# A fixed order table for every engine, and one store per output tile, in a gated-attention and token-mixer kernel

## The chip, the cores and the metric

The kernel runs on one core of a Trainium2 chip. The metric is device time in microseconds (us), taken as the median of several executions. A profile adds a span, which runs from the first to the last instruction and is 1.5 to 2 us shorter than the time. On one core, a run more than 1.5% above the fastest of the same kernel is called slow, and ratios use fast runs alone.

Five engines appear in the traces: PE (matrix products, with its weight loads as PEld), DVE (VectorE), ACT (ScalarE), POOL (GpSimd) and SP, which only issues transfers. The program gives each engine its own list of instructions, in a fixed order; an instruction that waits holds up those listed after it. In the trace of the kernel before, ACT idles 2.11 us until an alpha load has landed at 39.6 us, and a copy listed after the operation that needs it starts only at 40.08 us, though the transposes that it reads ended on PE at 38.6 us.

## The reference, cut to what matters

```python
# attention: 4 batches, 8 heads, 768 steps, head size 48; all float32
for t in range(S):
    state = alpha[:, :, t, :, None] * state + np.einsum('bhd,bhe->bhde', k[:, :, t], v[:, :, t])
    y[:, :, t] = np.einsum('bhd,bhde->bhe', q[:, :, t], state)
# mixer on x = y as (4, 768, 384); w_tok 768x256 and 256x768, w_ch 384x1536 and 1536x384
h = np.maximum(x.transpose(0, 2, 1) @ w_tok1, 0.0) @ w_tok2
u = x + h.transpose(0, 2, 1)
out = u + np.maximum(u @ w_ch1, 0.0) @ w_ch2          # (4, 768, 384), float32
```

## The kernel before

The recurrence is computed in 12 blocks of 256 steps (`n` = 0 to 11, three to a batch). Every block loads four 384 KB tiles (alpha, k, q, v). Two neighbouring steps lie in one partition of a load, so a 128-row output tile comes out with the even rows in partitions 0 to 63 and the odd rows in partitions 64 to 127. The store has to undo that.

The program is built as a list of operations with names, possible engines, assumed durations and predecessors. `Plan.once` simulates them with a priority rule and thereby fixes the order on each engine, the engine where there is a choice (DVE or POOL, ACT or DVE), and the buffers:

```python
kk = O("kk", either(dve(768), pool_tt(768)), 5, writes=[pkk], reads=[kt, IE], ...)   # k times decay
trq = O("trq", pe([64] * 8), 8, writes=[bq], reads=[pkq], preds=[qq], emit=lambda e: g.tr(bq, pkq), mode="R")
evq = O("evq", either(dve(1024, True), act(1024)), 9, writes=[tpq], reads=[bq], ...) # copy out of PSUM
# ... t1, t2: token layer; up, ut: transpose of u; c1, c2: channel layer, 288 matmuls of 384 columns each
oo = P.op(f"o_{b}_{i}", dve(384), ..., writes=[o_], reads=[bank, us[i][0]], preds=[prev],
          emit=lambda e, i=i, bank=bank, o_=o_: g.oadd(o_, bank, us[i][0]))
P.op(f"st_{b}_{i}", {"SP": (350.0, 350.0)}, ..., reads=[o_], preds=[oo], emit=lambda e, i=i, o_=o_: g.store(o_, b, i), ...)

def store(self, o, b, i):
    dst = self.out[b, i * 128 : (i + 1) * 128, :].rearrange("(t s) d -> s t d", s=2)
    for h in range(2):
        self.nc.sync.dma_start(dst[h], self.t(o)[64 * h : 64 * h + 64, :])
```

There are three output buffers (`"o": 3`). Input loads and output stores are issued from SP, and weights, which are cast to bf16 on the way, from POOL.

## Time and profile before

| | value |
|---|---|
| time | 191.56 us (189.38 to 192.55, 3 runs) |
| span of the profiled run | 190.1 us |
| PE, DVE, ACT, POOL busy | 86%, 59%, 53%, 19% |
| first channel matmul | 40.9 us |
| last matmul starts | 184.8 us |

The first lines are from the page of the kernel before. The engine line gives busy us and instructions. The lines of digits show the busy share of each fortieth of the span in tenths, for PE, for PE's granted clock and for the transfer engines. The next two lines give the shares of the chain of work that ended last. Then come the group of output adds, with what the engine waited for just before them, and the stores with their time from issue to landing.

```profile
PE 164.0 (86%) x2489; PEld 101.7 (53%) x2489; DVE 112.8 (59%) x197; ACT 101.2 (53%) x200; POOL 35.9 (19%) x43
...
PE   0578578769999988977999999989999999999990
...
PEclk9999999978999999999999999999999999999997
DMA  5999999999999998999100123110001132000243
...
PE 62%; DMA 16%; SPq 10%; DVE 6%; ACT 2%; issue 2%; DVEq 0%; ACTq 0%
PE ps L794 26%; PE ps L799 21%; DMA at<-in_alpha_dram 14%; SPq L562 10%; PE ps L617 7%; PE ps L770 3%; DMA out_dram<-o 2%; DVE u L779 2%; PE ps L775 2%; PE ps L673 2%; DVE pkk L658 1%; DVE pkq L658 1%; DVE o L803 1%; PE ps L786 1%; DVE gtm 
...
L803 DVE TENSOR_TENSOR o<-ps,u 128x384 f32<-128x384 f32 x24 | 13.1, 555 | 38.1 <-PE ps L799 36.2
...
out_dram<-o SPq DMA_DIRECT2D x48, 96.0 KB, 2.2
...
```

PE is the engine that the chain runs through, and it is nearly full from the tenth slice on. The output adds wait 1.8 us for stores in the whole run, and a 96 KB store lands 2.2 us after its issue. The stores cost little here.

Two pieces of the chain of work of the kernel before follow, in order of time (start, length, what):

```profile
20.53 19.10 DMA at<-in_alpha_dram
...
40.91 4.11 PE ps L794 x15
...
```

An alpha load issued at 20.5 us lands at 39.6 us behind the weights. The channel matmuls (L794) start at 40.9 us.

The stretch view (busy us of PE, PEld, DVE, ACT and POOL, each with its count; granted clock; share of the 16 transfer engines; GB/s) over the last stores of the kernel before:

```profile
177.00:189.00 12.00, 8.11 (x50) 4.68 (x48) 3.03 (x6) 0.00 (x0) 0.00 (x0) 0.93 0.41 98
...
```

A share of 0.41 is 6.6 of the 16 transfer engines on average, while stores come in bursts.

### The profile page before, as it was taken

The page shows a single profiled execution, that of the slowest core. Times are in us where ns is not written, and L with a number is a line of the kernel's source. Part 1 is how long each engine was busy: PE and PEld are TensorE (multiplying, and loading weights), DVE is VectorE, ACT ScalarE, POOL GpSimd, SP SyncE. Part 2 cuts the span into 40 slices and gives each one's busy share as a digit, 9 for nine tenths or more (in the row PEclk, how much of TensorE's full clock was granted, in tenths as well). Part 3 has the DMA queues.
Part 4 walks back from the last instruction along what each step waited for, and adds up shares of the span by engine and source line. Part 5 has one row for each costly group of instructions (what it writes and reads, how often), then busy time and mean ns, then how long its engine had stood idle before and what let it go on. Part 6 is the DMA issues. An engine that isn't in the chain of part 4 may idle for free.

```text
span 190.1 us, 5770 instructions
## 1 busy us (share of the span) xinstructions
PE 164.0 (86%) x2489; PEld 101.7 (53%) x2489; DVE 112.8 (59%) x197; ACT 101.2 (53%) x200; POOL 35.9 (19%) x43
## 2 busy tenths in 40 slices
PE   0578578769999988977999999989999999999990
PEld 0357354445566544644566656655656566656650
DVE  3386996993598954869782672894724728100230
ACT  3655536456998624783985212679872121895000
POOL 4023980030431221255200000090000000000000
PEclk9999999978999999999999999999999999999997
DMA  5999999999999998999100123110001132000243
GB/s 156 322 320 270 240 209 207 205 203 270 283 295 247 288 299 229 298 264 269 47 3 3 41 54 75 41 47 5 3 0 40 46 86 71 12 3 0 65 100 83
DMA packets 57625, 27.11 MB, mean 143 GB/s; under 512 B 50816, under 2 KB 57600, under 8 KB 57600
## 3 DMA queue, kind: packets, MB, share of 16 engines
q1 hardware_dynamic: 53760, 23.60, 48.3%
q0 software_dynamic: 3840, 3.15, 10.3%
q8 instruction: 19, 0.31, 0.7%
q14 instruction: 6, 0.05, 0.1%
HBM read 25.17 MB, written 4.72 MB: 157 GB/s over the span
## 4 chain that ended last, share of the span: by engine, by line
PE 62%; DMA 16%; SPq 10%; DVE 6%; ACT 2%; issue 2%; DVEq 0%; ACTq 0%
PE ps L794 26%; PE ps L799 21%; DMA at<-in_alpha_dram 14%; SPq L562 10%; PE ps L617 7%; PE ps L770 3%; DMA out_dram<-o 2%; DVE u L779 2%; PE ps L775 2%; PE ps L673 2%; DVE pkk L658 1%; DVE pkq L658 1%; DVE o L803 1%; PE ps L786 1%; DVE gtm L698 1%
## 5 line engine op out<-in xcount | busy, mean ns | idle before, releaser
L794 PE MATMUL ps<-ut,wc 128*128 128x384 bf16 x288 | 52.8, 333 | 3.3 <-DVE o L803 1.4
L799 PE MATMUL ps<-wc,rt 128*128 128x384 bf16 x288 | 52.5, 327 | 0.0
L765 ACT ACTIVATE rt<-ps 128x384 bf16<-128x384 f32 x93 | 45.1, 490 | 10.9 <-PE ps L794 10.6
L794 PEld LDWEIGHTS <-wc 128*128 128x128 bf16 x288 | 26.9, 99 | 21.5 <-issue 3.7
L799 PEld LDWEIGHTS <-rt 128*128 128x128 bf16 x288 | 26.8, 98 | 17.2
L803 DVE TENSOR_TENSOR o<-ps,u 128x384 f32<-128x384 f32 x24 | 13.1, 555 | 38.1 <-PE ps L799 36.2
L698 DVE TENSOR_TENSOR gtm<-ps,mk 128x1024 bf16<-128x1024 f32 x24 | 28.5, 1218 | 2.3 <-PE ps L617 2.2
L779 DVE TENSOR_TENSOR u<-ps,x 128x384 bf16<-128x384 f32 x24 | 12.7, 552 | 2.0 <-PE ps L775 2.0
L602 POOL TENSOR_TENSOR at<-at 128x384 f32<-128x384 f32 x6 | 6.0, 996 | 33.8 <-DMA at<-in_alpha_dram 22.2
L683 ACT CAST x<-ps 128x384 bf16<-128x384 f32 x16 | 7.2, 479 | 8.1 <-PE ps L617 8.1
L617 PE MATMUL ps<-la,u 128*128 128x384 bf16 x18 | 6.5, 432 | 5.8 <-ACT la L611 5.2
L658 DVE TENSOR_TENSOR pkq<-qt,E 128x768 bf16<-128x768 f32 x10 | 11.0, 1097 | 1.0 <-ACT E L636 1.0
L658 DVE TENSOR_TENSOR pkk<-kt,IE 128x768 bf16<-128x768 f32 x8 | 8.3, 1033 | 4.7 <-ACT IE L642 4.5
L770 PE MATMUL ps<-x,wt 128*128 128x384 bf16 x48 | 10.6, 355 | 0.0
L775 PE MATMUL ps<-ht,wt 128*128 128x384 bf16 x48 | 9.8, 326 | 0.4 <-ACT ht L765 0.4
L673 PE MATMUL ps<-idn,pkk 64*128 64x64 bf16 x192 | 5.5, 202 | 5.4 <-DVE pkk L658 3.1
L617 PE MATMUL ps<-tpq,tpk 48*64 48x128 bf16 x384 | 9.6, 242 | 0.4 <-DVE tpq L685 0.4
L658 POOL TENSOR_TENSOR pkq<-qt,E 128x768 bf16<-128x768 f32 x2 | 3.6, 1810 | 31.8 <-PE ps L673 31.8
L617 PEld LDWEIGHTS <-tpk 48*64 48x64 bf16 x384 | 7.2, 121 | 3.8 <-issue 1.3
L617 PE MATMUL ps<-vb,gtm 64*128 64x48 bf16 x384 | 7.8, 186 | 1.6 <-DVE gtm L698 1.5
L658 POOL TENSOR_TENSOR pkk<-kt,IE 128x768 bf16<-128x768 f32 x4 | 7.2, 1811 | 10.0 <-ACT IE L642 10.0
L765 ACT ACTIVATE ht<-ps 128x384 bf16<-128x384 f32 x7 | 3.4, 490 | 10.5 <-PE ps L770 10.5
(77 smaller groups left out, 194.4 us busy)
## 6 DMA issues: line engine op xcount, KB each, us to landing
at<-in_alpha_dram SPq DMA_DIRECT2D x12, 384.0 KB, 5.3
kt<-in_k_dram SPq DMA_DIRECT2D x12, 384.0 KB, 5.4
qt<-in_q_dram SPq DMA_DIRECT2D x12, 384.0 KB, 5.3
vt<-in_v_dram SPq DMA_DIRECT2D x12, 384.0 KB, 5.2
out_dram<-o SPq DMA_DIRECT2D x48, 96.0 KB, 2.2
wc<-in_moe_w_ch_dram POOLq DMA_DIRECT2D x3, 384.0 KB, 12.6
wc<-in_moe_w_ch_dram POOLq DMA_DIRECT2D x2, 576.0 KB, 16.4
wt<-in_moe_w_tok_dram POOLq DMA_DIRECT2D x2, 192.0 KB, 6.9
```

The costliest lines, as they stand in the source:

```text
L562: self.ins[id(v)] = self.nc.sync.dma_start(self.t(v), src)
L617: return self.pe.matmul(out, lhsT=lhsT, rhs=rhs, start=start, stop=stop, skip_group_check=True)
L658: self.eng[e].tensor_tensor(self.t(dst)[:, :, :, 0:D], self.t(src).rearrange("p h s d -> p s h d"), bass.AP(tensor=f.tensor, offset=f.offs ...
L673: self.pe.transpose(o[:, c * 64 : c * 64 + 64], s[ph, c % 2, c - c % 2 : c - c % 2 + 2, :], self.idn[ph, ph])
L698: self.nc.vector.tensor_tensor(self.t(gtm)[:, sl, :, :], self.pair(gp).rearrange("p a (j t) -> p (a j) t", t=128), bass.AP(tensor=m.tensor ...
L765: self.act.activation(d, s, AF.Relu)
L770: self.pe.matmul(self.bank(bank)[:, 0:HD], lhsT=self.wt1[:, kc, m * 128 : m * 128 + 128], rhs=self.t(x), start=(kc == 0), stop=(kc == NS - 1))
L775: self.pe.matmul(self.bank(bank)[:, 0:HD], lhsT=self.wt2[:, kc, i * 128 : i * 128 + 128], rhs=self.t(hts[kc]), start=(kc == 0), stop=(kc = ...
L779: self.nc.vector.tensor_tensor(self.t(u), self.bank(bank)[:, 0:HD], self.t(x), ALU.add)
L794: self.pe.matmul(self.bank(bank)[:, 0:HD], lhsT=self.wc1[:, kc, mc * 128 : mc * 128 + 128], rhs=self.t(ut)[:, kc, half * 384 : half * 384 ...
L799: self.pe.matmul(self.bank(bank)[:, 0:HD], lhsT=self.t(rts[mc][0])[:, i * 128 : i * 128 + 128], rhs=self.wc2[:, mc, :], start=(mc == 0), s ...
L803: self.nc.vector.tensor_tensor(self.t(o), self.bank(bank)[:, 0:HD], self.t(u), ALU.add)
```

## The change

The intent is to replace the scheduler by the result of a search made offline over measured durations. A table names every operation in order and its engine by one letter. `decode` only assigns buffers. Three other things change in the same diff: the weights are released by the 10th load instead of the 11th or 12th, the first token weight becomes two operations, and the store becomes one transfer.

```diff
-    def run(self):
-        ... # simulate with priorities, choose order and engines
+    def run(self, order):
+        by = {o.name: o for o in self.ops}
+        self.order = [by[n] for n, _ in order]
+        for n, e in order:
+            by[n].on = e
+        ... # decode: buffers only
 ...
-    weight("wt1", 0, 1, 786432, gates[NB - 1]["qt"], -70000.0)
+    for p in range(2):
+        weight("wt1", p, 2, 393216, gates[NB - 1]["kt"], -70000.0 + p)
 ...
+ENGINES = {"t": "PE", "s": "ACT", "v": "DVE", "g": "POOL", "y": "SP"}
+ORDER = """
+ld_at0y ln0s cumw0t IE0s E0s ld_kt0y kk0v trk0t ld_qt0y ld_at1y ln1s ld_vt0y vb0s K0t qq0g trq0t Et0s s0_0v
+... # 839 operations
+c2_3_5_0t c2_3_5_1t st_2_5y c2_3_5_2t c2_3_5_3t o_3_5v st_3_5y c2_3_4_1t c2_3_3_3t o_3_3v st_3_3y
+c2_3_4_2t c2_3_4_3t o_3_4v st_3_4y
+"""
 ...
     def store(self, o, b, i):
         dst = self.out[b, i * 128 : (i + 1) * 128, :].rearrange("(t s) d -> s t d", s=2)
-        for h in range(2):
-            self.nc.sync.dma_start(dst[h], self.t(o)[64 * h : 64 * h + 64, :])
+        self.nc.sync.dma_start(dst, self.t(o))
 ...
-    plan = build(g)
-    order = plan.run()
+    order = build(g).run([(x[:-1], ENGINES[x[-1]]) for x in ORDER.split()])
```

## The prediction

> **What bounds the kernel now.** TensorE, after a slow start. By the page's table of engines PE is busy 86% of the 190.1 us span, DVE 59%, ACT 53%. In the chain of waits PE holds 62%, but its first 40.9 us are DMA issue (10%), a 19.1 us alpha load (landing at 39.6) and short ACT pieces. Only then does the first channel matmul (L794) start. From 40.9 to 185.1 us PE runs nearly without a break; output add and store end the span. Three terms: start of channel matmuls (40.9), dense PE stretch (144.2), tail (5.0).
>
> **Inside the dense stretch.** Warm 384-column matmuls start 163 ns apart; from 40.9 to 43.5 us, 320 ns. [...] Cost: 1.3 us. In the PE timeline, start-to-start gaps above 0.15 us sum to about 6.5 us in the rest: 1.84 at 70 (a state fence behind an ACT Ln waiting for alpha), 0.67 at 81, 1.61 at 85 (DVE waits for an output store to free its buffer), smaller ones at 89, 122-126, 161.
>
> **Removed or added.** Nothing on PE: counts match. Stores become one 192 KB transfer instead of two (24 fewer SP issues, near 0.6 us each). So whatever is gained must be idle PE time.
>
> **Start.** [...] the slices show DMA saturated from 5 to 88 us, and load issues between 22 and 41 us take 6-7 us each while weights pass. The change gates weights on the 10th load instead of the 11th/12th (1.2-2.5 us earlier), but puts alpha 3, q 3, alpha 4 ahead of wt2 and the channel weights, as POOL products stand before those issues in its in-order stream. The ACT Ln that held the ut copy behind an alpha landing is served early; wt2's permutation moves to POOL. First channel weights: issued about 26 us, landing (10.7 us at least before, fewer ahead now) at 33-36. I put the first L794 at 35 us: gain 6.
>
> **Dense stretch.** Reordered ACT/DVE heads should remove half of the 6.5 us; new waits will appear at 60-70 us, because block 5's inputs cannot land before about 55 while PE arrives 6 us earlier. Gain 3, range -1 to 5.
>
> **Tail.** One last store instead of two: 0.6.
>
> Sum 9.6 us, all on the critical path. Loads do not bind late: they end near 88 and two batches of mixer work (about 28.7 us each) follow.
>
> **Prediction:** 191.56 - 9.6 - about 2 for a search tuned on such traces = 180.0 us, range 174.0 to 186.5. Chances: faster by over 2% 0.93, within 2% 0.06, slower 0.01.
>
> **What would show it.** Right: first L794 at 33-37 us, last matmul near 175, PE busy near 90%, POOL busy up from 36 to about 57 us, no DVE wait on stores, no fence wait, 2-3 us of new PE waits at 60-70, DMA saturated to about 85. Wrong: L794 still near 40 (wc1 late, or v 3 delayed by weights, holding ht on ACT), or gaps over 5 us at 60-90.
>
> **What would make it wrong.** A fixed order stalls wherever the chip is later than assumed: one late DMA blocks a whole engine. POOL and DVE two-input operations slow each other (DVE scaling 0.95 us alone, 1.38 and 2.22 beside POOL); more POOL work could lengthen the early chain.

The sum: 6 + 3 + 0.6 = 9.6 us. The 1.3 us is worked out from the two spacings before it: 2.6 us at 320 ns hold what takes 1.3 us at 163 ns; it is not in the sum. "Warm" means a granted clock of 1.00; from 40.9 to 43.5 us it is 0.50. One measured case of the late DMA at the end is the wait of ACT given above (2.11 us). For "slow each other", POOL's share is that its product of k and alpha takes 1.70 us at 24.7 us, beside DVE's product of 2.22 us, and about 1.00 us in the three other cases.

## The result and the profile after

The changed kernel takes 226.36 us (225.78 to 227.89, 4 runs) against 191.25 us before (4 runs, of which one, 192.55, counts as slow). The ratio is 1.1887, with a 95% interval of 1.1771 to 1.2002: it is 19% slower. Ratios here and below are the mean time of one kernel's fast runs over that of the other's of the same rounds, so they are not quite the ratio of the quoted medians.

The same lines of the page, for the changed kernel:

```profile
PE 167.8 (75%) x2489; PEld 104.4 (46%) x2489; DVE 130.3 (58%) x223; ACT 80.3 (36%) x156; POOL 55.2 (25%) x61
...
PE   0485898999999949899499299999999398470000
...
PEclk9999999999999996999979979999999679796555
DMA  6999999999466766647313001100011100101111
...
PE 43%; DMA 24%; DVE 11%; SPq 6%; issue 4%; POOL 3%; ACT 3%; POOLq 0%; DVEq 0%
PE ps L813 15%; DMA out_dram<-o 13%; PE ps L808 12%; PE ps L631 8%; DMA kt<-in_k_dram 6%; DMA qt<-in_q_dram 3%; SPq L579 3%; PE ps L789 3%; SPq L611 3%; DVE gtm L712 2%; DMA vt<-in_v_dram 2%; PE ps L784 2%; PE ps L800 2%; PE ps L687 2%; DVE
...
L817 DVE TENSOR_TENSOR o<-ps,u 128x384 f32<-128x384 f32 x24 | 13.2, 554 | 43.8 <-DMA out_dram<-o 34.5
...
out_dram<-o SPq DMA_DIRECT2D x24, 192.0 KB
...
```

Nothing was added on PE: the same 2489 matmuls are busy for 167.8 us. The slices are 5.6 us long here and 4.8 us before. From 28 to 79 us (the sixth to the fourteenth slice) PE is busy 49.2 us, against 45.8 us before in the same time. Then holes appear, the first in the fifteenth slice, and the last four slices hold no PE work at all. The granted clock falls too: after the first hole, which ends at 84.1 us, it is 0.50 from 84.4 to 87.8 us. The other holes of over 3 us end at 110.1, 128.3, 178.2 and 194.1 us, and near the end of each the clock is 0.50 as well (111.7 to 115.1, 128.8 to 132.2, 176.5 to 183.4 and 193.6 to 197.0 us). That is one reason why PE is busy longer: in the trace of the kernel before, 384-column matmuls start 320 ns apart at 0.50 and 163 ns apart at 1.00. DVE's output adds now wait 34.5 us for output stores (1.8 before), and stores are 13% of the chain. L817, L813 and L808 are the lines that were L803, L799 and L794.

Pieces of the chain of work of the changed kernel near its end:

```profile
171.07 6.46 DMA out_dram<-o
...
187.46 9.85 DMA out_dram<-o
...
199.12 13.23 DMA out_dram<-o
...
```

DVE's output adds at the end of the changed kernel (start, length, engine, what, and in brackets the idle time before and what ended it):

```profile
204.62 0.56 DVE L817 TENSOR_TENSOR o<-ps,u 128x384 f32<-128x384 f32 x1 [6.67 <-DMA out_dram<-o]
208.52 0.56 DVE L817 TENSOR_TENSOR o<-ps,u 128x384 f32<-128x384 f32 x1 [3.34 <-DMA out_dram<-o]
212.44 0.56 DVE L817 TENSOR_TENSOR o<-ps,u 128x384 f32<-128x384 f32 x1 [3.36 <-DMA out_dram<-o]
```

With three output buffers, an add has to wait for the store three tiles earlier. The adds come 3.90 and 3.92 us apart, so 192 KB leave every 3.9 us. The stretch view of the changed kernel over this time:

```profile
205.00:224.00 19.00, 0.00 (x0) 0.00 (x0) 1.30 (x3) 0.00 (x0) 0.00 (x0) 0.50 0.13 49
...
```

The core moves 49 GB/s and keeps 0.13 of 16 engines busy, which is 2.1 engines. The stores are serial at two engines' rate, whatever PE does.

Earlier in the run, three input loads stand in the chain of the changed kernel:

```profile
83.56 7.47 DMA kt<-in_k_dram
...
102.58 5.18 DMA kt<-in_k_dram
...
116.44 7.25 DMA qt<-in_q_dram
...
```

Before, the input loads landed in a median of 5.2 to 5.4 us, most of them in slices where the transfer engines are at digit 9. Here the last q load needs 7.25 us, at a time when the transfer engines do little else but stores. The packet records of the trace show where the time goes. A load has 1024 packets of 384 B and a store has 128 packets of 1536 B:

| us from the start | 384 B packets started (q load) | 1536 B packets started (stores) | engines busy |
|---|---|---|---|
| 117 to 120 | 896 | 64 | 5.1, 17.0, 6.7 |
| 120 to 122 | 0 | 60 | 2.2, 2.0 |
| 122 to 124 | 128 | 4 | 2.3, 0.9 |

(The busy figure is the packet time started in each us divided by 1 us, so it can pass 16.) Fourteen sixteenths of the load (896 of 1024) are through by 120 us. The last two sixteenths (128) start only when the store is nearly finished. The trace does not record which engine a packet ran on, so it is inferred, not shown, that they belong to the two engines on which the store lies ahead of them. Packets of 4 B close each part: fourteen of them start from 119.1 to 119.7 us, two at 122.1 us when the store's last data packets have started, and two near 123.4 us at the end of the load. That each engine works off the transfers of one queue in their order is inference from these counts.

How many engines a store used is told by the same packets. In the kernel before, 48 loads and 48 stores leave 1536 packets of 4 B on this queue, 16 for each transfer. In the changed kernel, 48 loads and 24 stores leave 816, which is 16 for a load and 2 for a merged store. That there is one for each engine used is inferred; it agrees with the share of 0.13 (2.1 engines) and with the packets in flight at once: at most 3 from 205 to 224 us in the changed kernel, and 17 from 177 to 189 us in the kernel before. The same count gives 4 for a store in e4 and 16 in e3 and e5 below (53088, 53376 and 53376 packets on the queue, of which 52224 carry data and 768 belong to the loads). The merged store has a source of 128 partitions and a target of 2 by 64 by 384; each of the two old stores has 64 rows on both sides. The prediction did not ask how many engines a store uses.

### The profile page after: what moved, and what is told of

Read it like the earlier page. It is cut to its first block, busy times and chain, and to the rows that moved or that the text cites. A ratio compares the mean times of both kernels' runs of the same rounds, so it can differ in the third digit from the quotient of the medians.

```text
span 225.0 us, 5711 instructions
## 1 busy us (share of the span) xinstructions
PE 167.8 (75%) x2489; PEld 104.4 (46%) x2489; DVE 130.3 (58%) x223; ACT 80.3 (36%) x156; POOL 55.2 (25%) x61
## 4 chain that ended last, share of the span: by engine, by line
PE 43%; DMA 24%; DVE 11%; SPq 6%; issue 4%; POOL 3%; ACT 3%; POOLq 0%; DVEq 0%
PE ps L813 15%; DMA out_dram<-o 13%; PE ps L808 12%; PE ps L631 8%; DMA kt<-in_k_dram 6%; DMA qt<-in_q_dram 3%; SPq L579 3%; PE ps L789 3%; SPq L611 3%; DVE gtm L712 2%; DMA vt<-in_v_dram 2%; PE ps L784 2%; PE ps L800 2%; PE ps L687 2%; DVE kt L664 2%
## 5 line engine op out<-in xcount | busy, mean ns | idle before, releaser
L813 PE MATMUL ps<-wc,rt 128*128 128x384 bf16 x288 | 59.2, 350 | 7.8 <-DVE o L817 7.8
L808 PE MATMUL ps<-ut,wc 128*128 128x384 bf16 x288 | 55.4, 334 | 1.6 <-DVE rt L781 1.6
L813 PEld LDWEIGHTS <-rt 128*128 128x128 bf16 x288 | 28.8, 103 | 28.5 <-issue 13.3
L779 ACT ACTIVATE rt<-ps 128x384 bf16<-128x384 f32 x48 | 22.1, 490 | 49.8 <-PE ps L808 49.6
L817 DVE TENSOR_TENSOR o<-ps,u 128x384 f32<-128x384 f32 x24 | 13.2, 554 | 43.8 <-DMA out_dram<-o 34.5
L808 PEld LDWEIGHTS <-wc 128*128 128x128 bf16 x288 | 27.4, 99 | 20.4 <-issue 3.9
L781 DVE TENSOR_SCALAR rt<-ps 128x384 bf16<-128x384 f32 x48 | 24.5, 548 | 5.5 <-PE ps L808 5.4
L672 POOL TENSOR_TENSOR pkq<-qt,E 128x768 bf16<-128x768 f32 x7 | 13.9, 1988 | 6.2 <-ACT E L656 5.4
L741 POOL TENSOR_TENSOR ss<-tmp,E 128x192 bf16<-128x192 f32 x9 | 4.7, 524 | 26.8 <-DVE tmp L738 25.5
L697 ACT COPY tpk<-ps 128x1024 bf16<-128x1024 bf16 x7 | 7.1, 1011 | 11.4 <-PE ps L687 11.3
L668 POOL TENSOR_TENSOR qt<-qt,lf 128x384 f32<-128x384 f32 x6 | 6.2, 1028 | 17.7 <-DMA qt<-in_q_dram 17.7
L664 DVE TENSOR_TENSOR kt<-kt,at 128x384 f32<-128x384 f32 x6 | 6.8, 1135 | 5.0 <-DMA kt<-in_k_dram 5.0
```

Of the source, the lines that this page charges most:

```text
L664: self.eng[e].tensor_tensor(a, a, self.t(at)[:, :, 1, :], ALU.mult)
L672: self.eng[e].tensor_tensor(self.t(dst)[:, :, :, 0:D], self.t(src).rearrange("p h s d -> p s h d"), bass.AP(tensor=f.tensor, offset=f.offs ...
L779: self.act.activation(d, s, AF.Relu)
L781: self.nc.vector.tensor_scalar_max(d, s, 0.0)
L808: self.pe.matmul(self.bank(bank)[:, 0:HD], lhsT=self.wc1[:, kc, mc * 128 : mc * 128 + 128], rhs=self.t(ut)[:, kc, half * 384 : half * 384 ...
L813: self.pe.matmul(self.bank(bank)[:, 0:HD], lhsT=self.t(rts[mc][0])[:, i * 128 : i * 128 + 128], rhs=self.wc2[:, mc, :], start=(mc == 0), s ...
```

## The experiments

Each table row is measured against the kernel before on the same chip in the same rounds. "Last PE" is the start of the last matmul of the profiled run. Medians are over all runs and ratios over fast ones; two of the four runs of e1 and one each of e5 and e10 were slow, so the ratio of e1 rests on two fast runs. The runs marked "1 run" have no ratio.

| run | what | median us | ratio to before (95%) | first channel matmul | last PE | span |
|---|---|---|---|---|---|---|
| before | | 191.56 | | 40.9 | 184.8 | 190.1 |
| changed | table, one store on 2 engines | 226.36 | 1.1887 (1.1771 to 1.2002) | 39.3 | 200.7 | 225.0 |
| e1 | table, two stores | 186.29 | 0.9601 (0.953 to 0.9672) | 40.7 | 179.7 | 185.8 (slow) |
| e2 | old scheduler, store on 2 engines | 219.71 | 1.1433 (1.1388 to 1.1477) | 42.6 | 197.9 | 217.6 |
| e3 | table, one store on 16 (wrong rows) | 180.22 | 0.9384 (0.934 to 0.9427) | 40.3 | 173.4 | 177.8 |
| e4 | table, one store on 4 (wrong rows) | 200.43, 1 run | | 39.6 | 187.1 | 198.7 |
| e5 | table, natural rows, one store on 16 | 179.89 | 0.936 (0.931 to 0.9411) | 39.5 | 174.8 | 178.5 |
| e6 | e5 without the permuting copy | 179.03 | 0.9346 (0.9304 to 0.9388) | 38.1 | 172.9 | 176.6 |
| e7 | table, two stores, SP and ACT | 184.46 | 0.9614 (0.9561 to 0.9668) | 39.2 | 179.4 | 183.7 |
| e8 | table, two stores, 5 buffers | 183.08 | 0.9556 (0.9496 to 0.9617) | 40.5 | 176.6 | 182.2 |
| e9 | old scheduler, natural rows, one store | 190.35 | 0.9956 (0.9891 to 1.0022) | 41.4 | 185.6 | 189.3 |
| e10 | e1, last q load moved up | 182.88 | 0.9549 (0.9485 to 0.9613) | 41.7 | 176.9 | 183.0 (slow) |
| e11 | e6, q load moved up, 5 buffers | 178.19 | 0.9331 (0.9287 to 0.9375) | 38.3 | 172.9 | 176.6 |
| e12 | changed, last q load moved up | 222.47, 1 run | | 40.5 | 197.7 | 220.8 |

### Store or table

The theory (S) was that the shape of the merged store is the cause. The rival (O) was that the table's order does not suit the chip: loads stand behind stores in SP's in-order queue, and POOL has more work.

e1, the changed kernel with the old store:

```diff
-        self.nc.sync.dma_start(dst, self.t(o))
+        for h in range(2):
+            self.nc.sync.dma_start(dst[h], self.t(o)[64 * h : 64 * h + 64, :])
```

> The changed kernel with its order table untouched, but each output tile stored again as two transfers of 64 rows. Theory S (the merged store, whose target has an outermost dimension of 2, runs on 2 of the 16 DMA engines, takes about 4 us per 192 KB, holds the output buffers and the input loads queued behind it): about 180 us (176 to 185), at most 17 packets in flight at the end instead of 3, DVE's wait on output stores below 3 us instead of 34.5. Rival O (the order table itself is bad on the chip: loads standing behind stores in SP's in-order queue, more work on POOL): still above 215 us.

(The 17 and the 3 packets in flight are the counts given above, from the traces of the kernel before and of the changed kernel.)

It measured 186.29 us (184.5 in its two fast runs), 4% faster than before. The group of output adds of e1:

```profile
L818 DVE TENSOR_TENSOR o<-ps,u 128x384 f32<-128x384 f32 x24 | 13.2, 553 | 18.4 <-DMA out_dram<-o 11.2 <-PE ps L814 7.2
...
```

Their wait on stores fell from 34.5 to 11.2 us. That is much better, but not the "below 3 us" that was expected. (This profile is of a slow run.) So S is right about the main cause, and about 4.5 us is left between the fast runs and the expected 180.

e2, the kernel before with the merged store (the reverse of the edit above, on the old scheduler):

> The kernel before with nothing changed but the store merged as in the change. Theory S: 24 stores of about 4 us each, the last six alone 23 us from about 178 us on, so 200 to 215 us. Rival O: within 2% of before, as only 24 issues are saved.

It measured 219.71 us, ratio 1.1433, which is 4.7 us above the expected range. The group of output adds of e2:

```profile
L802 DVE TENSOR_TENSOR o<-ps,u 128x384 f32<-128x384 f32 x24 | 13.2, 555 | 56.2 <-PE ps L798 35.9 <-DMA out_dram<-o 20.2
...
```

The adds wait 20.2 us for stores, against 1.8 us before. The store alone, without the table, costs 28 us. Rival O is out as the main cause.

e3, the changed kernel with one store whose target rows are viewed as 16 by 8. The rows land in a wrong order on purpose, and the result was wrong (relative error 1.3):

```diff
-        dst = self.out[b, i * 128 : (i + 1) * 128, :].rearrange("(t s) d -> s t d", s=2)
+        dst = self.out[b, i * 128 : (i + 1) * 128, :].rearrange("(t s) d -> s t d", s=16)
```

> The changed kernel with one 192 KB store per tile as in the change, but with the 128 rows of the target viewed as 16 by 8 and not 2 by 64 (rows land in a wrong order on purpose, so the result is wrong). Theory S: the outermost dimension decides, so about 179 us (175 to 185), within 2% of the run with two stores. Rival B (a transfer of 192 KB is too large, or one store per tile is late whatever its shape): above 210 us.

It measured 180.22 us. Bytes, number of transfers, issuer, order and buffers are those of the changed kernel; only the outermost dimension differs, and 46 us are gone. From the page of e3:

```profile
PE 158.2 (89%) x2489; PEld 101.0 (57%) x2489; DVE 127.8 (72%) x223; ACT 80.6 (45%) x156; POOL 57.0 (32%) x61
...
L817 DVE TENSOR_TENSOR o<-ps,u 128x384 f32<-128x384 f32 x24 | 13.2, 553 | 16.0 <-PE ps L813 10.8
...
out_dram<-o SPq DMA_DIRECT2D x24, 192.0 KB, 2.6
...
```

The 192 KB store lands in 2.6 us. PE is busy 89% of a span of 177.8 us. This run was within 2.4% of e1, not within 2%, and on the faster side.

e4, the same with 4 by 32 (`s=4`, again wrong rows):

> As the run before, the 128 rows viewed as 4 by 32 (wrong rows on purpose). Theory S: 4 DMA engines, a store in about 2 us, moved at about 100 GB/s; time between that of 16 and that of 2, near 185 us (178 to 200). Rival B: as slow as the changed kernel, above 210 us.

It measured 200.43 us, a single run, just above the expected range. The last output adds of e4, and its stretch view over them:

```profile
187.05 0.56 DVE L817 TENSOR_TENSOR o<-ps,u 128x384 f32<-128x384 f32 x1 [4.92 <-DMA out_dram<-o]
189.00 0.56 DVE L817 TENSOR_TENSOR o<-ps,u 128x384 f32<-128x384 f32 x1 [1.39 <-DMA out_dram<-o]
190.96 0.56 DVE L817 TENSOR_TENSOR o<-ps,u 128x384 f32<-128x384 f32 x1 [1.40 <-DMA out_dram<-o]
```

```profile
187.00:198.00 11.00, 0.47 (x3) 0.08 (x1) 1.68 (x3) 0.00 (x0) 0.00 (x0) 0.68 0.24 84
...
```

The adds now come 1.95 us apart, half of the 3.9 us with two engines, and 0.24 of 16 engines is 3.8. Outermost 2, 4 and 16 give 226, 200 and 180 us. The outermost dimension of the store, and with it the number of transfer engines, decides.

### Where the 47 us of span went

With the same table, the run with two engines and the run with sixteen (e3) can be compared milestone by milestone:

| milestone | changed, us | e3, us | difference |
|---|---|---|---|
| first token matmul of batch 1 | 65.7 | 66.0 | -0.3 |
| first token matmul of batch 2 | 118.3 | 107.4 | 10.9 |
| last matmul starts | 200.7 | 173.4 | 27.3 |
| end of the span | 225.0 | 177.8 | 47.2 |

Until the first stores (issued from 59.4 us on) they are alike. Then, by the chain above, loads behind stores and adds without buffers cost PE 10.9 us by the start of batch 2; how much each of the two costs was not separated. Another 16.4 us are lost up to the last matmul, and 19.9 us in the tail, when only stores are left.

e12 measures one piece of it: the changed kernel with the last q load ahead of the stores that it stood behind. (The table has three there, `st_1_2`, `st_1_1` and `st_1_3`; the expectations of e10 and e12 say four.)

```diff
-... ld_kt11y ia7t ...  st_1_2y ... st_1_1y ... st_1_3y ld_qt11y q0r11g ...
+... ld_kt11y ld_qt11y ia7t ...  st_1_2y ... st_1_1y ... st_1_3y q0r11g ...
```

> The changed kernel with its two-engine store, and the last q load moved ahead of the four stores. How much of the loss is that load behind slow stores: its 7.3 us landing and PE's 4.2 us gap at 124 us should go, 220 to 223 us. If the queue order were the main cause: below 200 us.

It measured 222.47 us, one run, inside the expected range. PE's gap at 124 us (4.0 us idle, 4.2 us from start to start) is gone. The place of this one load is worth some 4 us, and the other 42 us to e3 stay. The k load issued at 83.56 us, right behind a store, was not moved.

### A correct store on 16 engines

e5 brings the rows into natural order where q is copied out of PSUM after its transposes, so that an output tile is 128 consecutive rows. The mask is built for natural columns, the first token weight loads in natural order, and the copy of the second token weight, which used to permute it, only copies.

```diff
     def trev(self, e, d, bp):
+        nat = len(d.shape) == 4                                   # q, not k
 ...
+        if nat:
+            d = d.rearrange("p f (j t s) -> p f j t s", j=4, s=2)
+            src = src.rearrange("p f (j s t) -> p f j t s", j=4, s=2)
 ...
-                             pattern=[[-1, 2], [1, 2], [2, 64]], channel_multiplier=-2)
+                             pattern=[[-1, 2], [1, 128]], channel_multiplier=-2)
 ...
-        self.nc.sync.dma_start(dst, self.t(o))
+        self.nc.sync.dma_start(self.out[b, i * 128 : (i + 1) * 128, :], self.t(o))
```

> The changed kernel with its table, rows brought into their natural order when q is copied out of PSUM after its transposes, so that an output tile is 128 consecutive rows and one store has 128 as the outermost dimension; token weights then load in natural order. Result correct. Theory S (the number of DMA engines of the store is what mattered): within 1.5% of the wrong-row run with 16 (180.2 us), so 177.5 to 183. Against it: the copy reads PSUM with a stride and may be slower on VectorE (12 copies, of which 7 there), so above 184 if that is on the critical path.

The result is correct and takes 179.89 us, as expected. The seven copies of q on DVE rose from 0.69 to 1.22 us each; the five on ACT stayed at 1.01 us. In e9 below, with the same edit, the eight copies on DVE take 1.22 us too (0.69 before). The copy now reads with a step of 64 elements where it read neighbours; that this step is the cause is inference. PE, the bound engine, does not notice: the time equals that of e3.

e6 also removes the copy of the second token weight from POOL and loads the weight in place:

> As the run before, and the permuting copy of the second token weight on GpSimd, no longer needed, taken out (the weight is loaded in place). Expected 0 to 2 us faster than the run before, 176 to 181: token matmuls of batch 0 wait less, but the start is bound by the attention chain of block 2 and by k of block 3, so near 0.

It measured 179.03 us, not told apart from e5 (the intervals overlap). But the trace shows a piece of which the prediction had warned ("more POOL work could lengthen the early chain") without putting it into its sum. In the changed kernel, around 30 us (start, length, engine; timeline):

```profile
29.79 1.59 POOL L699 COPY wt<-ut 128x768 bf16<-128x768 bf16 x2
...
30.62 2.95 DVE L664 TENSOR_TENSOR kt<-kt,at 128x384 f32<-128x384 f32 x1
...
31.35 1.80 POOL L672 TENSOR_TENSOR pkq<-qt,E 128x768 bf16<-128x768 f32 x1
...
```

and in e6:

```profile
29.75 1.82 POOL L667 TENSOR_TENSOR pkq<-qt,E 128x768 bf16<-128x768 f32 x1
...
30.54 1.45 DVE L659 TENSOR_TENSOR kt<-kt,at 128x384 f32<-128x384 f32 x1
...
```

The DVE product of k and alpha takes 0.55 us as a rule (the median of six in the changed kernel). Here it takes 2.95 us: it starts at 30.62 us, during the weight copy of POOL (two instructions, 29.79 to 31.38 us), and ends at 33.57 us, 0.42 us after the q product, which POOL had started later, at 31.35 us. In e6, with only the q product, it takes 1.45 us and again ends 0.42 us after that product (31.99 and 31.57 us). It looks as if DVE's product did its work only after POOL's, and lost the turn to the q product as well; the two traces show the times, not the cause. The first channel matmul moved from 39.5 us (e5) to 38.1 us (e6); in e11, which also lacks the copy, it starts at 38.3 us.

e9 is the old scheduler with natural rows and the 128-row store (the same edits on the kernel before):

> The kernel before with its own scheduler, and only rows in natural order and one 128-row store per tile. It splits the gain of the natural-row version of the changed kernel (0.936 of before) into store and table. If the table is what gains: 187 to 191 us, 0.975 to 1.0 of before. If fewer and whole stores gain most of it: below 184 us.

It measured 190.35 us, ratio 0.9956 with an interval that holds 1. A good store alone gains nothing that can be told from before. So the 6.4% that e5 gains need the table. The two do not simply add: the table with two stores gains 4% (e1), the good store on the old order 0.4%, both together 6.4%.

### Why two stores stay above one

e1 was expected at 180 and came at 184.5 in fast runs, e3 at 180.2. Three runs looked for the cause: one for the issue time on SP, one for output buffers, one for the last q load.

e7 issues the second half from ACT:

```diff
-        for h in range(2):
-            self.nc.sync.dma_start(dst[h], self.t(o)[64 * h : 64 * h + 64, :])
+        for h, q in enumerate((self.nc.sync, self.nc.scalar)):
+            q.dma_start(dst[h], self.t(o)[64 * h : 64 * h + 64, :])
```

> The changed kernel with two 64-row stores, one issued from SP and one from ScalarE's queue. Theory I (what keeps two stores from SP above the single 16-engine store, 186.3 against 180.2, is 24 more issues of 0.6 us in SP's in-order queue): 179 to 183 us. Rival (ScalarE, in order, is held by each store's wait): 184 or more.

It measured 184.46 us, so this test speaks for the rival, though only by half a microsecond. SP has the shorter list, and the tail from the last matmul's start falls to 4.3 us, as with one store (6.1 us in e1). But PE now waits 0.9 and 1.5 us for ACT (the `rt` tiles), and the time does not follow.

e8 gives the outputs five buffers for three. Others get fewer in exchange: `x` 14 to 12, `u` 13 to 12, `ht` 4 to 3.

> The changed kernel with two 64-row stores from SP and 5 output buffers for 3 (paid for by 2 x, 1 u and 1 ht buffer). Theory I (issue in SP): DVE's wait on stores falls from 11 us to under 6, time 183 to 187, as the last twelve issues still take over 7 us. Rival (too few output buffers): 179 to 182.

It measured 183.08 us. It lies in the range expected if issuing on SP is the limit, where e7 had spoken against that. No output add waits for a store any more (11.2 us in e1), and yet the time moves little. Buffers alone are not it.

e10 moves the last q load ahead of the stores, as e12 does, on e1:

> The changed kernel with two 64-row stores, and in the table only the last q load moved ahead of the four stores that it stood behind on SP. Theory L (the 2.9 us gap of PE at 114 us, which the two-store runs have and the 16-engine runs have not, is this load waiting behind stores): the gap falls below 0.6 us and the time to 180 to 183 us (before: 186.3, 184.5 in fast runs). Rival (the gap has another cause, the issue time of stores elsewhere): 184 or more and the gap stays.

It measured 182.88 us. PE's wait at 114 us (2.7 us idle, 2.9 us from start to start) is gone, as expected; the largest left nearby is 0.6 us at 118 us. (e7 and e8 still have this wait, 2.7 and 3.0 us.) But the interval overlaps that of e1, and the profiled run was a slow one. So the gap has its cause, while the 4 us between one and two stores are not settled: part is the tail, which takes 5.6 to 6.1 us from the last matmul's start in e1, e8 and e10 (e1 and e10 profiled in slow runs) and 4.4 us in e3, and the rest is spread over gaps that no single edit removes. More buffers and the moved load were not tried together on two stores.

### The best version

e11 is e6 with the last q load moved and five output buffers:

> Natural rows, no permuting copy, the last q load ahead of the stores, 5 output buffers for 3 (2 x, 1 u and 1 ht buffer fewer). PE gaps left in the dense stretch that these touch: 0.9 us at 157 (output buffers), 0.5 us at 104 to 114. Expected 177 to 179 us, 0 to 1.5 us under the run without the last two edits (179.0).

It is correct and takes 178.19 us (177.93 to 178.72), ratio 0.9331. Its interval overlaps that of e6, so the two last edits are not shown to help. From the page of e11:

```profile
PE 158.4 (90%) x2489; PEld 101.7 (58%) x2489; DVE 129.9 (74%) x223; ACT 80.1 (45%) x156; POOL 54.5 (31%) x59
...
PE   0387389999899999999999999989999999999992
...
PEclk9999999999999999999999999999999999999998
...
L817 DVE TENSOR_TENSOR o<-ps,u 128x384 f32<-128x384 f32 x24 | 13.1, 553 | 14.1 <-PE ps L813 14.0
...
```

It beats both kernels: 7% under the one before, 21% under the changed one.

## Why the prediction was wrong, point by point

- **"Stores become one 192 KB transfer instead of two (24 fewer SP issues, near 0.6 us each). So whatever is gained must be idle PE time."** This is the step that failed. The store was costed by its issues and bytes, not by the engines that it would use. In the changed kernel a store takes 3.9 us on two engines, 94 us for 24 (24 times 3.9), in a queue that loads share, and output adds wait 34.5 us for it. e3 changed only the outermost dimension and gave 46 us back; e2 put the store into the old kernel and lost 28 us.
- **Tail: "One last store instead of two: 0.6."** The tail from the last matmul's start to the end grew from 5.3 to 24.3 us. With 16 engines it is 4.4 us (e3), so a gain of 0.9 us was there to be had.
- **"no DVE wait on stores, no fence wait".** The first is wrong: 34.5 us, and 0 us only with five buffers and stores on 16 engines (e8, e11). The fence wait near 72 us (1.68 us before) is gone: in the changed kernel, e1, e3, e5, e6 and e11 PE waits nowhere more than 0.4 us between 55 and 75 us.
- **"Loads do not bind late: they end near 88."** In the kernel before, the last packets of the loads start at 89.5 us, but here the last q load was issued at 116.4 us, behind stores, and landed at 123.7 us. The table itself puts it late: it is issued at 105.8 us in e3 too, where stores on 16 engines do not hold it up.
- **Start: "first L794 at 35 us: gain 6".** It came at 39.3 us, a gain of 1.6 us, and at 40.3 us in e3. The prediction's own sign of error ("L794 still near 40") was right. One part of the cause, which it had named as a risk but not counted, is the product of k and alpha on DVE beside two POOL operations, 2.95 us for 0.55. e6 removed one of them, and the start moved by 1.4 us, to 38.1 (one profile each). What keeps it from 35 beyond that stays open.
- **Dense stretch: "Gain 3, range -1 to 5".** The mechanism (reordered heads remove waits) was right, but it is less than half of what was gained. Between the first channel matmul and the start of the last one the old kernel takes 143.9 us (184.8 - 40.9) and e3 133.1 (173.4 - 40.3): 10.8 us. By the stretch view over these times, PE's idle time fell from 5.3 to 1.0 us, which is 4.2 us and close to the forecast. The other 6.6 us lie in PE's busy time, which shrank from 138.6 to 132.1 us for the same matmuls. About 1.5 us of that can be the clock (an estimate: the trace of the kernel before grants 0.50 from 40.9 to 44.0 us, that of e3 1.00 throughout); what the rest is stays open. So "whatever is gained must be idle PE time" failed here as well. The new waits feared at 60 to 70 us did not come.
- **"POOL busy up from 36 to about 57 us"** was right (55.2). "PE busy near 90%" holds for e3 (89%), not for the changed kernel (75%).
- The sum, 180.0 us, is what the table gives with a store on 16 engines (e3 180.22, e5 179.89). That is partly luck: of the span, e3 gains 0.6 us at the start (6 forecast), 10.8 in the dense stretch (3 forecast) and 0.9 in the tail (0.6 forecast).

## What to carry to other kernels

Before merging two transfers, look at the outermost dimension of the target: a view such as "even rows, then odd rows" has 2 there, and here about 2 of 16 transfer engines then did the work (0.13 of 16), while a load issued after it on that queue waited for its last two sixteenths (the last 128 of 1024 packets started from 122 us on, the first 896 by 120 us). Cost a transfer by bytes per engine used (192 KB left every 3.9 us with an outermost 2 and every 1.95 us with 4, and landed in 2.6 us with 16), and read the share of transfer engines in the stretch view (0.13 of 16 is two) when a store seems slow. When a change brings a new order together with a small edit, run the edit alone on the old order: here the small edit turned a gain of 4% (e1) into a loss of 19%.
